# Value-weight sums and second-block x sums traced behind the key products' outputs, and the last token group's residual added on VectorE with plain stores

## The chip, the cores and the metric

The kernel runs on one core of a Trainium2 chip. The metric is the time of one execution on the device, in microseconds (us). Times below are medians over executions. A ratio is the mean time of one kernel's fast runs over the mean of the other's fast runs of the same rounds, so it is not quite the ratio of the medians that are quoted. Each comparison has its 95% interval. An execution's time is longer than the span that its profile shows: by 1.7 us in before. Experiments 9 to 12 ran on another chip than experiments 1 to 8, each beside before.

## The reference, cut to what matters

```python
xn = _layernorm(x)                       # x: 2048 tokens x 1024
s = _A_ref(xn, wqkv, wo)                 # q, k, v projections; attention over 8 dilated keys; wo
g = _silu(_B_ref(xn, w1, w3, w2))        # gated MLP, 1024 -> 3584 -> 1024
return x + s * g
```

Everything outside is bfloat16. The change touches the key and value projections near the start, and `x + s * g` for the last 512 tokens (the last 256 of each of the last two chunks of 512) at the very end.

## The kernel before

Each large product is a 2x2 block product done with seven block products instead of eight. That needs sums of blocks of weights and of x, which VectorE makes beforehand, and sums of outputs, which VectorE makes while it takes the outputs out of PSUM. The kernel keeps four two-bank tiles in PSUM, so an output that is not taken out in time keeps a later product from getting its banks (below, ScalarE's copy waits for such banks until 67.33 us and PE waits 2.6 us for the copy).

```python
def seven(key, A, B, e11, e12, e22, e21, snap=None):
    ...
    pa = bank2(...); mm(pa, a11, b11)            # first product (none if snap holds it)
    pe = bank2(...); mm(pe, s1, t1)              # needs the first weight sum s1
    pb = bank2(...); act_copy(pb, pa)            # ScalarE; pb needs a free bank pair
    sp5 = k4(...);   act_copy(sp5, pe)
    mm(pa, a12, b21); e11(pa)                    # output on ScalarE
    flush()                                      # the leftover product of the group before
    mm(pb, s2, t2); su2 = k4(...); act_copy(su2, pb)
    mm(pe, s4, b22); e12(pe, su2)                # output on VectorE
    mm(pb, s3, t3);  e22(pb, sp5)                # output on VectorE
    pend.append(tail)                            # tail: mm(pb, a22, t4); e21(pb)
```

An output of the second token chunk goes to a buffer `pk` and from there to DRAM. `pk`, `sp5` and `su2` share one ring of four buffers:

```python
def park(t, c, j0, name):                        # t: 0 q, 1 k, 2 v;  c: token chunk
    tl = k4(name, (2, CH), BF16)
    dst = (q_dram, k_dram, v_dram)[t][c, :, j0:j0 + 2, :]
    def fin():
        nc.sync.dma_start(out=dst, in_=tl[:])
    return tl[:], fin

def qkv_copy(t, c, j0):                          # cut; for VectorE outputs:
    anchor["u"] = anchor.get("v")
    anchor["v"] = nc.vector.tensor_add(d, ps[:], a[0][:])
```

`behind(key)` makes the instruction that follows stand, on its own engine, behind the instruction noted under that key. The sums in question stood like this:

```python
def before_v(g):                                 # called after each of the two key groups
    if g > 0:
        return
    for h in I:
        qkv_load(2, h, wv[h])                    # 2 MB of value weights
    tr(3)                                        # transposes of the last x chunk, by DMA
    qkv_sums(*wv, sv)                            # four VectorE sums, need the value weights

qkv_seven(1, 0, wk0, wk1, sk, before_v, snap[2:4])
with behind("u"):
    xn_sums(xT1[0], xT1[1], xT1[2], xT1[3], xs1) # four VectorE sums of the second token block
...
qkv_seven(2, 0, *wv, sv, step)
```

At the end, the product with `wo` comes out in groups `(b, u, dh, gp)` of 256 tokens by 512 columns. The residual x had been copied to the output beforehand, and each group was added to it by an accumulating store on GpSimd's queue, all but one:

```python
def finished(b, u, dh, gp, ps, add=None):
    last = (b, u, dh, gp) == (1, 1, 0, 1)
    ...
    if last:
        for i in I:
            nc.vector.tensor_mul(g[:, i], ps[i], g[:, i])
            nc.vector.tensor_add(g[:, i], g[:, i], xw[0][:, i])
            nc.sync.dma_start(out=..., in_=g[:, i])
        return
    to_bf16(d, ps, add)
    anchor["v"] = nc.vector.tensor_mul(g, d, g)
    nc.gpsimd.dma_start(out=..., in_=g, accum_op=ALU.add)
```

## Time and profile before

| | before |
|---|---|
| median of the first 3 executions | 735.9 us (734.22 to 736.3) |
| span of the profiled execution | 735.9 us (its time: 737.58) |
| PE busy, VectorE busy | 718.5 us, 622.3 us |
| PE idle in 60-80 us, longest wait there | 2.6 us |
| last matmul's end to the end of the span | 8.8 us |

The page's busy line (engine, us, share of the span, instructions) says which engine bounds the kernel:

```profile
PE 718.5 (98%) x3367; PEld 345.9 (47%) x3367; DVE 622.3 (85%) x674; ACT 314.1 (43%) x327; POOL 103.2 (14%) x162
```

PE idles only 17.4 us in all, so a gain must come from those idle stretches, or from stretches in which PE is slow. The list of PE's waits (who waited for whom: us in total, times, longest) starts with the stall in question:

```profile
PE aq L149 <- ACT bq L159: 2.6, 1, 2.6
```

PE waited for ScalarE's copy of the first value product. Why was the copy late? VectorE's timeline around it shows that (start us, us, engine, line, operation, out<-in, count; in brackets the idle time before and what ended it). Lines L316 to L319 are the value sums, L351 the outputs of the key groups:

```profile
53.70 1.23 DVE L351 TENSOR_TENSOR pk<-bq,pq 128x1024 bf16<-128x1024 f32 x1 [0.46 <-PE bq L149]
61.36 1.23 DVE L316 TENSOR_TENSOR wring<-wring 128x2048 f16<-128x2048 bf16 x1 [6.43 <-DMA wring<-in_A_wqkv_dram]
62.62 1.23 DVE L317 TENSOR_TENSOR wring<-wring 128x2048 f16<-128x2048 f16 x1
63.76 1.22 DVE L319 TENSOR_TENSOR wring<-wring 128x2048 f16<-128x2048 bf16 x1
64.89 1.22 DVE L318 TENSOR_TENSOR h_sb<-wring 128x2048 f16<-128x2048 bf16 x1
66.03 1.22 DVE L351 TENSOR_TENSOR pk<-eq,uq 128x1024 bf16<-128x1024 f32 x1
```

PE had finished that `eq` product at about 60.6 us, but VectorE, which took its instructions in the program's order here, first sat 6.43 us waiting for the value weights and then made the four sums. The copy had to wait for the banks of `eq`; ScalarE's timeline names VectorE's output as what ended its wait:

```profile
67.33 1.00 ACT L159 COPY bq<-aq 128x1024 f32<-128x1024 f32 x1 [7.39 <-DVE pk L351]
```

PE's own timeline shows what followed:

```profile
62.13 1.89 PE L149 MATMUL aq<-xT,wring 128*128 128x512 bf16 x8
63.86 1.89 PE L149 MATMUL eq<-xs,wring 128*128 128x512 f16 x8
68.38 3.02 PE L149 MATMUL aq<-xT,wring 128*128 128x512 bf16 x8 [2.63 <-ACT bq L159]
71.19 2.49 PE L149 MATMUL bq<-xs,h_sb 128*128 128x512 f16 x8
```

After the wait, eight matmuls take 3.02 us, where 1.89 is usual. The windows view gives the granted clock of PE for each stretch, third column from the right:

```profile
66.00:68.00 2.00, 0.00 (x0) 0.00 (x0) 2.00 (x3) 0.67 (x1) 0.00 (x0) 1.00 0.73 162
68.00:70.00 2.00, 1.62 (x6) 0.84 (x6) 2.00 (x3) 1.27 (x2) 0.00 (x0) 0.75 1.02 410
70.00:72.00 2.00, 2.00 (x6) 0.73 (x5) 2.00 (x3) 0.57 (x1) 0.00 (x0) 0.50 1.04 395
72.00:74.00 2.00, 2.00 (x10) 1.13 (x9) 0.91 (x1) 0.73 (x2) 0.00 (x0) 0.90 1.05 415
```

The second place is the end. The timeline of the last 11 us, cut to the last matmuls, VectorE's last addition, the last accumulating stores (POOL) and the last plain ones (SPq), and then SyncE's wait before it closes the program:

```profile
724.84 2.51 POOL L952 DMA_DIRECT2D out_dram<-h_sb  x2 [3.23 <-DVE h_sb L951]
...
725.18 1.89 PE L149 MATMUL wb<-wring,oT 128*128 128x512 f16 x8
...
727.84 1.18 POOL L952 DMA_DIRECT2D out_dram<-h_sb  x1 [0.49 <-DVE h_sb L951]
727.94 1.37 SPq L948 DMA_DIRECT2D out_dram<-h_sb  x2
728.50 0.42 DVE L947 TENSOR_TENSOR h_sb<-h_sb,xw 128x512 bf16<-128x512 bf16 x1
```

```profile
SPq L1072 <- DMA out_dram<-h_sb: 4.7, 1, 4.7
```

All arithmetic is done at 728.9, and the span ends at 735.9: 7 us in which stores land and the program is closed.

### The profile page before, as it was taken

To read this page: it belongs to the slowest core of one execution; us is meant where nothing else is said; L and a number is where in the kernel's file an instruction comes from. 1 tells how busy PE (TensorE), PEld (TensorE's weight loads), DVE (VectorE), ACT (ScalarE), POOL (GpSimd) and SP (SyncE) were. 2 spreads that over 40 slices of the span, in tenths; PEclk is the share of its full clock that TensorE was granted. 3 is DMA by queue.
4 is the path that set the end of the run, shared out by engine and by line. 5 is a ranking of instruction groups with operands and counts; after the bars stand their busy time and mean duration, and the time that the engine had idled before them with its cause. 6 is when DMAs were issued, how large, how long until landed. Compare 5 with 4: busy or idle time off the path is not lost.

```text
span 735.9 us, 8786 instructions
## 1 busy us (share of the span) xinstructions
PE 718.5 (98%) x3367; PEld 345.9 (47%) x3367; DVE 622.3 (85%) x674; ACT 314.1 (43%) x327; POOL 103.2 (14%) x162
## 2 busy tenths in 40 slices
PE   8998999999999999999999999999999999999995
PEld 4654665654444444444444444444444444444442
DVE  8996298968798879878989899969859999979973
ACT  5743343446555545654545411124454555020332
POOL 0000000010410010142202010010334000410012
PEclk9999999999999999999999999999999999999998
DMA  9379438866646452467655745459799443754425
GB/s 336 121 187 325 188 145 262 266 204 211 182 162 200 131 185 86 140 190 242 228 172 190 239 158 198 159 180 370 178 282 324 147 135 103 229 183 144 156 26 88
DMA packets 117562, 140.82 MB, mean 191 GB/s; under 512 B 14225, under 2 KB 91025, under 8 KB 116881
## 3 DMA queue, kind: packets, MB, share of 16 engines
q1 hardware_dynamic: 103120, 100.68, 43.7%
q0 software_dynamic: 14400, 39.59, 18.0%
q8 instruction: 26, 0.43, 0.2%
q14 instruction: 16, 0.12, 0.0%
HBM read 98.30 MB, written 39.58 MB: 187 GB/s over the span
## 4 chain that ended last, share of the span: by engine, by line
PE 57%; DVE 19%; issue 14%; DMA 4%; ACT 3%; POOL 2%; POOLq 0%; SPq 0%; DVEq 0%; ACTq 0%
PE bm L149 16%; PE am L149 11%; PE em L149 11%; PE bq L149 6%; DVE pt L410 4%; PE aq L149 4%; PE eq L149 4%; DVE pt L412 2%; DMA wring<-in_A_wqkv_dram 2%; PE db L149 2%; DVE stats L249 1%; DMA t_dram<-wring 1%; PE wb L149 1%; DVE pt L414 1%; POOL out_dram L952 1%
## 5 line engine op out<-in xcount | busy, mean ns | idle before, releaser
L149 PEld LDWEIGHTS <-wring 128*128 128x128 f16 (+1 forms) x1920 | 201.7, 105 | 219.6 <-issue 8.8
L149 PEld LDWEIGHTS <-h_sb 128*128 128x128 f16 (+1 forms) x1088 | 114.1, 105 | 122.1 <-issue 1.7
L149 PE MATMUL bm<-xs,wring 128*128 128x512 f16 x504 | 117.3, 379 | 0.4 <-DVE h_sb L661 0.2
L149 PE MATMUL am<-xT,wring 128*128 128x512 bf16 x336 | 79.5, 379 | 0.2
L410 DVE TENSOR_TENSOR pt<-qt,kT 128x4096 bf16<-128x4096 bf16 x32 | 73.2, 2288 | 0.7
L149 PE MATMUL db<-wring,h_sb 128*128 128x512 f16 x336 | 73.2, 379 | 0.0
L465 DVE TENSOR_TENSOR BC<-Ep,vT 128x2048 bf16<-128x2048 bf16 x56 | 67.0, 1217 | 0.2
L646 DVE TENSOR_TENSOR um<-em,um 128x1024 f32<-128x1024 f32 x28 | 34.2, 1222 | 19.9 <-PE em L149 19.7
L648 ACT ACTIVATE g<-um 128x1024 bf16<-128x1024 f32 x28 | 29.6, 1057 | 49.7 <-DVE um L646 49.7
L149 PE MATMUL da<-wring,h_sb 128*128 128x512 bf16 x224 | 49.2, 379 | 0.0
L451 POOL DMA_DIRECT2D Ep<-pb x64 | 38.1, 603 | 25.4 <-DVE pb L447 18.5
L149 PE MATMUL bm<-h_sb,wring 128*128 128x512 f16 x168 | 39.7, 379 | 0.0
L149 PE MATMUL em<-xs,wring 128*128 128x512 f16 x168 | 39.7, 379 | 0.0
L149 PE MATMUL em<-xT,wring 128*128 128x512 bf16 x168 | 39.7, 379 | 0.0
L412 DVE TENSOR_TENSOR pt<-pt 128x2048 bf16<-128x2048 bf16 x32 | 39.1, 1221 | 0.5
L475 DVE TENSOR_TENSOR oT<-oT,BC 128x2048 bf16<-128x2048 bf16 x32 | 39.0, 1220 | 0.5
L159 ACT COPY bm<-am 128x1024 f32<-128x1024 f32 x28 | 28.0, 999 | 26.1 <-PE am L149 26.1
L159 ACT COPY pm<-em 128x1024 f32<-128x1024 f32 x28 | 28.4, 1013 | 19.2 <-PE em L149 19.2
L159 ACT COPY um<-bm 128x1024 f32<-128x1024 f32 x28 | 28.4, 1013 | 18.6 <-PE bm L149 18.1
L667 ACT CAST g<-bm 128x1024 bf16<-128x1024 f32 x28 | 28.3, 1010 | 17.6 <-PE bm L149 17.6
L351 DVE TENSOR_TENSOR pk<-eq,uq 128x1024 bf16<-128x1024 f32 x12 | 14.7, 1221 | 21.8 <-PE eq L149 14.1
L952 POOL DMA_DIRECT2D out_dram<-h_sb x15 | 18.8, 1387 | 97.9 <-DVE h_sb L951 97.7
(172 smaller groups left out, 976.3 us busy)
## 6 DMA issues: line engine op xcount, KB each, us to landing
wring<-in_B_w_dram SPq DMA_DIRECT2D x61, 512.0 KB, 4.1
wring<-t_dram SPq DMA_DIRECT2D x16, 512.0 KB, 4.4
t_dram<-wring POOLq DMA_DIRECT2D x14, 512.0 KB, 4.1
wring<-in_A_wqkv_dram SPq DMA_DIRECT2D x6, 1024.0 KB, 8.4
wring<-t_dram SPq DMA_DIRECT2D x16, 384.0 KB, 5.3
wring<-in_B_w_dram SPq DMA_DIRECT2D x12, 384.0 KB, 4.3
wring<-in_A_x_dram SPq DMA_DIRECT2D x16, 256.0 KB, 5.5
Ep<-pb POOLq DMA_DIRECT2D x64, 64.0 KB, 4.6
```

The costliest lines, as they stand in the source:

```text
L149: anchor["pe"] = nc.tensor.matmul(ps, lhsT=lhs[k], rhs=rhs[k], start=(first and k == 0), stop=(k == n - 1), skip_group_check=not first,)
L159: nc.scalar.copy(out=out_, in_=in_)
L351: anchor["v"] = nc.vector.tensor_add(d, ps[:], a[0][:])
L410: nc.vector.tensor_mul(p_t[:], q[:], kT[:, :, o:o + CH])
L412: nc.vector.tensor_add(p_t[:, 0:4, :], p_t[:, 0:4, :], p_t[:, 4:8, :])
L451: nc.gpsimd.dma_start(out=pr[c][r:P:NR, :, sq * P:(sq + 1) * P], in_=pb[sq * 32:(sq + 1) * 32, :, :])
L465: nc.vector.tensor_mul(dst, E[:, w, :].unsqueeze(1).to_broadcast([P, n, CH]), vT[:, js, o:o + CH])
L475: nc.vector.tensor_add(A, A, B if w0 else C)
L646: v = nc.vector.tensor_add(su2[:], pe[:], su2[:])
L648: nc.scalar.activation(out=hl["g"][:, :, CH:], in_=su2[:], func=ACTF.Silu)
L667: nc.scalar.copy(out=hl["g"][:, :, 0:CH], in_=pb[:])
L952: nc.gpsimd.dma_start(out=out_rows(out_flat, b, u, dh, gp), in_=g, accum_op=ALU.add)
```

## The change

It means to let VectorE take the second key group's outputs out of PSUM before it does anything that waits for the value weights, and to end the program without accumulating stores. The diff, cut to its core:

```diff
@@ spill stores of x and its sums (x_dram, xs_dram), from 65-75 us to 164-244 us
-                        nc.sync.dma_start(out=d, in_=f)
+                        with behind("sp"):
+                            nc.sync.dma_start(out=d, in_=f)
@@ before_v
-        if g > 0:
-            return
-        for h in I:
-            qkv_load(2, h, wv[h])
-        tr(3)
-        qkv_sums(*wv, sv)
+        if g == 0:
+            for h in I:
+                qkv_load(2, h, wv[h])
+            tr(3)
+        else:
+            with behind("v"):
+                qkv_sums(*wv, sv)
@@
-    with behind("u"):
-        xn_sums(xT1[0], xT1[1], xT1[2], xT1[3], xs1)
+    def step0(g):
+        if g == 0:
+            with behind("v"):
+                xn_sums(xT1[0], xT1[1], xT1[2], xT1[3], xs1)
+        w2_step()
-    qkv_seven(2, 0, *wv, sv, step)
+    qkv_seven(2, 0, *wv, sv, step0)
@@ finished; xw now holds the residual of four groups, and the copies of x to the output shrink to match
+            if b == 0 or gp == 0:
+                ... accumulating store on GpSimd's queue, as before
+            elif (u, dh) != (1, 0):
+                to_bf16(d, ps, add)
+                nc.vector.tensor_mul(g, d, g)
+                nc.vector.tensor_add(g, g, xw[u, dh])
+                nc.sync.dma_start(out=rows_, in_=g)
+            else:
                 for i in I:
-                    nc.vector.tensor_mul(g[:, i], ps[i], g[:, i])
-                    nc.vector.tensor_add(g[:, i], g[:, i], xw[0][:, i])
+                    if i == 0:
+                        nc.scalar.copy(out=d[:, i], in_=ps[i])
+                    nc.vector.tensor_mul(g[:, i], ps[i] if i else d[:, i], g[:, i])
+                    nc.vector.tensor_add(g[:, i], g[:, i], xw[u, dh][:, i])
```

More of the change, by code (lines that the diff above doesn't have):

```diff
@@ L865, in wo @@
         if b == 1:
-            xw[0] = k4("xw", (2, CH), BF16)
-            nc.sync.dma_start(out=xw[0], in_=out_rows(x_flat, 1, 1, 0, 1))
+            xt4 = att_tile((2, 2, 2, CH), BF16, "xw")
+            for u in I:
+                for dh in I:
+                    xw[u, dh] = xt4[:, u, dh]
+                    nc.sync.dma_start(out=xw[u, dh], in_=out_rows(x_flat, 1, u, dh, 1))
         def product(ps, gp, lhs, rhs, first):
@@ L927 @@
     xw = {}
-    copies = [((2 * b + u) * CH, CH, dh) for b in I for u, dh in ((0, 0), (1, 1), (0, 1), (1, 0)) if (b, u, dh) != (1, 1, 0)]
-    copies.insert(0, (3 * CH, 2 * P, 0))
+    copies = [((2 * b + u) * CH, CH // (1 + b), dh) for b in I for u, dh in ((0, 0), (1, 1), (0, 1), (1, 0))]
     def residual():
@@ L938, in finished @@
     def finished(b, u, dh, gp, ps, add=None):
-        last = (b, u, dh, gp) == (1, 1, 0, 1)
         g = g_tile(b, u, dh, gp)
@@ L942, in finished @@
         d = h_sb[:, 16 + 2 * n:18 + 2 * n, CH:]
+        rows_ = out_rows(out_flat, b, u, dh, gp)
         with hp():
-            if last:
-                for i in I:
-                    nc.vector.tensor_mul(g[:, i], ps[i], g[:, i])
-                    nc.vector.tensor_add(g[:, i], g[:, i], xw[0][:, i])
-                    nc.sync.dma_start(out=out_rows(out_flat, b, u, dh, gp)[:, i], in_=g[:, i])
-                return
-            to_bf16(d, ps, add)
-            anchor["v"] = nc.vector.tensor_mul(g, d, g)
-            nc.gpsimd.dma_start(out=out_rows(out_flat, b, u, dh, gp), in_=g, accum_op=ALU.add)
+            if b == 0 or gp == 0:
+                to_bf16(d, ps, add)
+                anchor["v"] = nc.vector.tensor_mul(g, d, g)
+                nc.gpsimd.dma_start(out=rows_, in_=g, accum_op=ALU.add)
+            elif (u, dh) != (1, 0):
+                to_bf16(d, ps, add)
+                nc.vector.tensor_mul(g, d, g)
+                nc.vector.tensor_add(g, g, xw[u, dh])
+                nc.sync.dma_start(out=rows_, in_=g)
+            else:
+                for i in I:
+                    if i == 0:
+                        nc.scalar.copy(out=d[:, i], in_=ps[i])
+                    nc.vector.tensor_mul(g[:, i], ps[i] if i else d[:, i], g[:, i])
+                    nc.vector.tensor_add(g[:, i], g[:, i], xw[u, dh][:, i])
+                    nc.sync.dma_start(out=rows_[:, i], in_=g[:, i])
     x_load(0)
@@ L1008, in before_v @@
     def before_v(g):
-        if g > 0:
-            return
-        for h in I:
-            qkv_load(2, h, wv[h])
-        tr(3)
-        qkv_sums(*wv, sv)
+        if g == 0:
[5 more added lines that the diff above has]
+                qkv_sums(*wv, sv)
     qkv_seven(1, 0, wk0, wk1, sk, before_v, snap[2:4])
-    with behind("u"):
-        xn_sums(xT1[0], xT1[1], xT1[2], xT1[3], xs1)
     step = lambda g: w2_step()
+    def step0(g):
[3 more added lines that the diff above has]
+        w2_step()
     pace["n"] = PACE[0]
-    qkv_seven(2, 0, *wv, sv, step)
+    qkv_seven(2, 0, *wv, sv, step0)
     pace["n"] = PACE[1]
```

## The prediction

> What bounds it now. TensorE. The page's busy table has PE at 718.5 of 735.9 us, so all PE idling is 17.4 us; VectorE is busy 622.3. A table of busy time by 20 us windows puts the idling at the ends and in one place: 3.4 us in 0-20, 2.6 in 60-80, 8.8 after 720, under 1 anywhere else.
>
> The stall at 66-68 us. In VectorE's timeline the sums of the value weights stand ahead of two evictions of the second key group. They wait for the value weights (idle 6.43 us, until 61.36), run four adds of 1.13 us, and only then is the first key output evicted (66.03). Its PSUM bank is what ScalarE's copy of the first value product needs (67.33), and PE waits 2.63 us for that copy. Afterwards PE is slow: eight matmuls take 3.02 us where 1.89 is usual, and the granted clock is 0.75 in 68-70, 0.50 in 70-72, 0.90 in 72-74. From the starts of the next groups this costs 1.7 us more. [...]
>
> What the change does there. By the instruction order, both key evictions now stand ahead of the value sums, and the second block's x sums (four adds) stand behind two value evictions. On PE the leftover key product moves ahead of the value product that needs the first sum. Expected: evictions at 60.6 and 62.3, the first sum at 63.5-64.7; PE works on the first value product until 63.9, on the leftover product until 65.6, then needs the sum, which is there. The stall and the slow clock go: 4.3 to 4.5 us, all on the critical path, since PE is busy without a gap for 80 us after it. The x sums are first read near 90 us and are not late at about 80. The spill stores of x and its sums leave 65-75 us, where DMA share is 1.02-1.05, for about 190-250 us, where it is about 0.6; I expect nothing of that on PE.
>
> The tail. The last matmul ends at 727.07, VectorE at 728.9; two last stores are issued at 727.94 and 729.0, and SyncE waits until 734.0. In between, three 256 KB accumulating stores keep DMA share at 1.1-1.2 (727-732) and the last store takes 4.9 us to land. The change makes three of the four last groups plain stores: their accumulates go, VectorE gets three more adds of about 0.6 us, ScalarE one copy. Adding up VectorE's queue from 722.1 (1.13 + 2x0.6 for evictions, 0.6 per product or sum), its end moves about 1 us later, to 729.9. But the last store then meets an almost empty queue: plain 256 KB stores land in 2.0-2.4 us at best in this trace. [...] Landing near 732.5 instead of 734.0: gain 1.4 us, uncertain by 0.8. The residual's 1 MB load waits only for the third chunk's last use of its buffer, near 651, and should delay no weights.
>
> Predicted: 735.9 - 4.4 - 1.4 = 730.1 us; 8 in 10 between 728.3 and 732.8. Faster by over 2%: 0.02; within 2%: 0.97; slower: 0.01.
>
> Shown right by: no PE wait for that ScalarE copy, granted clock 1.00 in 60-80, PE busy total near 717, no accumulating store in the last 10 us, last landing 3 us after VectorE's end.
>
> Wrong if: the value weights land later than 62 us; PE then waits for the first sum; evictions on VectorE push the last store past 731; the moved spills delay weights, or a later VectorE-bound stretch (420-490) swallows the lead.

No term of the sum rests on them: 735.9 - 4.4 - 1.4 = 730.1 us stands as recorded. The 4.4 is read from the profile of before (2.63 us of wait and 1.7 of slow matmuls). The 1.4 is an estimate from it: VectorE's queue added up, and the landings of plain 256 KB stores, whose fastest nine of 36 took 2.03 to 2.40 us (the stores of the key, query and value outputs).

## The result, and the profile after

| | before | after |
|---|---|---|
| median of 6 executions | 736.21 us (734.22 to 737.72) | 732.37 us (731.36 to 733.51) |
| ratio, 95% interval | | 0.9949 (0.9932 to 0.9966) |
| span of the profiled execution | 735.9 us | 730.3 us |
| last matmul's end to the end of the span | 8.8 us | 6.0 us |

The time, 732.4 us, lies inside the predicted range, near its upper end. The gain is 3.8 us where 5.8 was predicted. The two profiled spans differ by 5.6 us, so the pair of profiles flatters the change: the profiled execution of before took 737.58 us, 1.4 us above its median.

The busy line after. Some matmul records are missing from this trace (3312 of 3367), so PE's total is a little low:

```profile
PE 714.2 (98%) x3312; PEld 345.8 (47%) x3367; DVE 624.2 (85%) x677; ACT 314.5 (43%) x328; POOL 99.3 (14%) x159
```

The wait for ScalarE's copy is gone from the list of PE's waits, and a small one is new:

```profile
PE bq L149 <- DVE pk L351: 0.3, 1, 0.3
```

VectorE's timeline has the order that was wanted, both key outputs ahead of the value sums. But look at the brackets: neither output started when PE was done. Both waited for a DMA, a store of an earlier key output:

```profile
62.13 1.23 DVE L351 TENSOR_TENSOR pk<-eq,uq 128x1024 bf16<-128x1024 f32 x1 [6.35 <-DMA k_dram<-pk]
63.93 1.23 DVE L351 TENSOR_TENSOR pk<-bq,pq 128x1024 bf16<-128x1024 f32 x1 [0.58 <-DMA k_dram<-pk]
65.07 1.22 DVE L316 TENSOR_TENSOR wring<-wring 128x2048 f16<-128x2048 bf16 x1
```

And PE's timeline. In before, eight such matmuls took 1.73 us from their start to that of the next eight (62.13 to 63.86). By that measure the first value product (`aq`, 62.98) should end 1.73 us after its start, at 64.71; four matmuls of the leftover product start at 65.21, 0.50 us late, and should end 0.86 us later, at 66.07; the next product starts at 66.35, when the first sum is ready, 0.28 us late:

```profile
62.98 1.89 PE L149 MATMUL aq<-xT,wring 128*128 128x512 bf16 x7
65.21 1.02 PE L149 MATMUL bq<-xs,h_sb 128*128 128x512 f16 x4 [0.34 <-DVE pk L351]
66.35 1.92 PE L149 MATMUL eq<-xs,wring 128*128 128x512 f16 x8
```

The granted clock stays at 1.00 (windows view, same columns):

```profile
66.00:68.00 2.00, 1.89 (x10) 0.95 (x9) 1.97 (x3) 0.00 (x0) 0.00 (x0) 1.00 0.95 264
68.00:70.00 2.00, 2.00 (x11) 1.32 (x10) 1.82 (x2) 1.02 (x1) 0.00 (x0) 1.00 0.87 85
70.00:72.00 2.00, 2.00 (x11) 1.09 (x10) 0.00 (x0) 1.93 (x2) 0.00 (x0) 1.00 1.03 388
```

At the end, VectorE finishes 2.8 us after PE (1.9 before), but SyncE waits only 1.2 us for landings, in three pieces (timeline and SyncE's waits):

```profile
722.41 1.89 PE L149 MATMUL wb<-wring,oT 128*128 128x512 f16 x8
...
722.99 3.50 SPq L955 DMA_DIRECT2D out_dram<-h_sb  x3
...
726.34 0.75 DVE L961 TENSOR_TENSOR h_sb<-h_sb,xw 128x512 bf16<-128x512 bf16 x2
726.82 0.84 SPq L962 DMA_DIRECT2D out_dram<-h_sb  x2
```

```profile
SPq L1086 <- DMA out_dram<-h_sb: 1.2, 3, 0.6
```

To compare kernels stretch by stretch, I took five numbers from each trace. A: start of the first query product. B: from the first value product to the first gate product of the MLP, the stretch that holds the stall. C: from there to the first product of the last output stage. D: from the last matmul's end to the end of the span. The last column is the time at half clock before the end. The text below refers to this table.

| profile | A | B | C | D | half clock |
|---|---|---|---|---|---|
| before | 12.41 | 102.15 | 538.4 | 8.81 | 3.41 |
| before, run again | 12.44 | 102.07 | 539.1 | 8.67 | 3.41 |
| new tail only | 12.38 | 100.36 | 539.1 | 6.09 | 0 |
| before without three accumulating stores | 12.71 | 99.76 | 538.6 | 4.68 | 0 |
| later spill stores only | 13.22 | 100.25 | 538.9 | 8.92 | 0 |
| new order only | 13.28 | 99.97 | 539.3 | 7.92 | 0 |
| value sums moved only | 13.04 | 105.12 | 538.3 | 8.50 | 6.83 |
| after | 13.25 | 98.47 | 538.4 | 5.98 | 0 |
| after, run again | 12.91 | 98.88 | 539.6 | 5.97 | 0 |
| after, two additions on GpSimd | 13.32 | 98.84 | 538.6 | 8.16 | 0 |
| after, two stores on GpSimd's queue | 12.92 | 108.28 | 538.6 | 6.08 | 10.24 |
| after, outputs in own memory | 13.57 | 97.73 | 539.2 | 5.96 | 0 |
| the same, old spill stores | 13.30 | 97.72 | 538.5 | 6.08 | 0 |
| the same as own memory, one accumulating store back | 14.00 | 97.72 | 538.6 | 5.76 | 0 |

C varies by 1.3 us among profiles of kernels that are nearly the same there. One profile can't settle a difference of 1 us in the total; B and D are steadier.

### The profile page after: what moved, and what is told of

It reads as the page before. It is cut to its first block, busy times and chain, and to the rows that moved or that the text cites. A ratio compares the mean times of both kernels' runs of the same rounds, so it can differ in the third digit from the quotient of the medians.

```text
span 730.3 us, 8739 instructions
## 1 busy us (share of the span) xinstructions
PE 714.2 (98%) x3312; PEld 345.8 (47%) x3367; DVE 624.2 (85%) x677; ACT 314.5 (43%) x328; POOL 99.3 (14%) x159
## 4 chain that ended last, share of the span: by engine, by line
PE 71%; DVE 18%; DMA 4%; issue 3%; ACT 3%; SPq 1%; POOL 0%; DVEq 0%; ACTq 0%; POOLq 0%
PE bm L149 17%; PE am L149 11%; PE em L149 11%; PE db L149 7%; PE bq L149 5%; PE de L149 4%; DVE pt L410 4%; PE eq L149 4%; PE da L149 3%; PE aq L149 3%; PE wb L149 2%; DVE pt L412 2%; PE we L149 2%; PE wa L149 2%; DMA q_dram<-pk 1%
## 5 line engine op out<-in xcount | busy, mean ns | idle before, releaser
L661 DVE TENSOR_TENSOR h_sb<-bm,pm 128x1024 bf16<-128x1024 f32 x21 | 25.6, 1218 | 5.3 <-PE bm L149 5.3
```

The source lines that it names most:

```text
L661: anchor["v"] = nc.vector.tensor_add(h[:, :, CH:], pb[:], sp5[:])
```

## The experiments

### 1. Before, run again

No edit. It measures how much executions of one program differ.

> The program of before, under another label: it measures how far executions of one program differ, and gives a second profile of it. Theory A (the profiled run of before was a dear one): its 2.63 us stall let the granted clock fall to one half for some 3 us[...]. Then the ratio is 1.000, the mean granted clock differs between executions (0.994 in the first profile, about 0.997 where the clock held) and the time with it by 1 to 2 us. Theory B (the clock falls in every execution): clock 0.994 in all, and times within 0.5 us for the same clock.

(What A expects is that the clock falls in only part of the executions.)

Measured: 737.87 us against 736.84, ratio 1.0004 (0.9983 to 1.0025). The six executions had mean granted clocks from 0.993 to 0.997, and in three jobs together before ran 39 times with its clock listed. In 13 of them the clock was 0.995 or lower, with a mean time of 738.06 us; in 26 it was higher, with 736.06 us. Part of the clock figure comes from the idle end of the program (half clock from 731.2 to 735.9 us in the profile of before), so the two groups may overlap at 0.996. The share of low clocks differs by job: 8 of 17 and 4 of 11 in two jobs on one chip, 1 of 11 in the third, on another chip. The second profile fell into the low group like the first: its trace has one period of half clock near 68 us, 3.413 us long to the nanosecond, as in the first. Three other programs with the same order of VectorE's key and value work (new tail only, no accumulating stores, later spills only) had none in their profiles, although PE waited for the same copy. Without the fall, B is 100.1 us on the mean of those three; with it, 102.1. So an execution with the fall takes 2.0 us longer, and the fall came in about a third of the executions of before. The half clock itself is not all of it: B less PE's wait is 99.52 and 99.15 us with the fall and 97.83 or 97.84 in the three without, so the half clock costs 1.3 to 1.7 us, and the rest is that the stall was longer in the two (2.8 us on the mean, against 2.3). Theory A holds.

PE was idle for 2.63 and 2.92 us in the two profiles where the clock fell, and for 1.92, 2.42 and 2.53 us in the three where it held. Both half-clock periods were 3.413 us long. Whether the length of the gap or something else decides can't be told from five profiles.

### 2. The new order alone

Edit: the first three hunks of the diff above on the kernel before, with the old tail.

> The reordered sums and the later spill stores alone, with the tail of before. From the two profiles the stretch from 50 to 75 us became 3.7 us shorter. If that part is worth the same in every execution: 732.5 us against 736.2 of before (ratio 0.995), nearly the whole of the measured 3.8 us, and the tail would be worth nothing. If the clock fell only in part of the executions of before, it is worth about 2 us (ratio 0.9973). PE should show the short waits of the changed kernel near 65 us (0.5 and 0.3 us) and the clock 1.00 in 60-80.

Measured: 736.26 us against 736.84, ratio 0.9987 (0.9967 to 1.0008): about 1 us, less than either guess, though the interval holds both no gain and the second guess (0.9973). The clock held, as expected (0.996 to 0.998 in all six). But PE's wait for the eviction was 1.6 us in this profile, where it was 0.3 in the profile of the whole change, so B was 99.97 and not 98.5. This made the wait for the earlier stores' landings a suspect: it differs from run to run, and so do the landings: the two stores landed 8.76 and 5.29 us after their issue in before, 7.88 and 5.88 in after.

### 3. The new tail alone

Edit: the last hunk of the diff alone, with the old order.

> The new tail alone, with the old order of the sums. In the two profiles the time from PE's last matmul to the end went from 8.8 to 6.0 us. Theory: the three accumulating stores kept the queues full and the last store late, so this holds in every execution: 2.8 us less (ratio 0.9962), VectorE's end 2.8 us after PE's, the last stores landing in about 1.8 us. Rival: the 4.9 us landing of before was that one run's luck, and 1 to 1.5 us (ratio 0.998 to 0.9985) is what the tail is worth. The stall at 66 us must stay at about 2.6 us.

Measured: 735.13 us against 736.84, ratio 0.9968 (0.9945 to 0.9992), about 2.4 us. D fell to 6.09 us, VectorE ended 2.80 us after PE and the stall was 2.5 us. The ratio's interval holds the rival's 0.998 too; what the rival falls by is D, which is 7.9 to 8.9 us in five profiles with the old tail. With experiment 2, the parts add up to 3.3 us, against 3.8 for the whole, inside the intervals.

### 4. Two outputs in memory of their own

Edit, on the kernel after: the two outputs that waited go to a piece of `oT` that is idle then, not to the ring of four buffers.

```diff
-        tl = k4(name, (2, CH), BF16)
+        if (t, c) == (1, 1) and j0 in (2, 6):
+            tl = oT[:, 0, j0 // 3:j0 // 3 + 2, :]
+        else:
+            tl = k4(name, (2, CH), BF16)
```

> The changed kernel, with the two key results that waited for the landing of two earlier key stores written to a piece of memory of their own (idle at that time) in place of the ring of four buffers. Theory: those landings held both evictions up by 0.7 us and cost PE 0.5 us before the leftover key product and 0.3 us before the product that needs the first value sum. Then VectorE evicts within 0.1 us of PE, both PE waits go, and the kernel is 0.7 us faster than the changed kernel: about 731.7 against 736.2 of before (ratio 0.9939). Rival: the first sum then waits for the weights' landing instead, and PE's waits stay at 0.5 us or more.

Measured: 732.71 us against 736.84, ratio 0.9933 (0.9913 to 0.9952). VectorE's timeline now shows both outputs waiting for PE alone, and PE's shows the three groups back to back (63.30, 65.03, 65.92):

```profile
61.85 1.23 DVE L354 TENSOR_TENSOR oT<-eq,uq 128x1024 bf16<-128x1024 f32 x1 [5.75 <-PE eq L149]
63.50 1.23 DVE L354 TENSOR_TENSOR oT<-bq,pq 128x1024 bf16<-128x1024 f32 x1 [0.43 <-PE bq L149]
64.64 1.22 DVE L316 TENSOR_TENSOR wring<-wring 128x2048 f16<-128x2048 bf16 x1
```

```profile
63.30 1.89 PE L149 MATMUL aq<-xT,wring 128*128 128x512 bf16 x7
65.03 1.03 PE L149 MATMUL bq<-xs,h_sb 128*128 128x512 f16 x4
65.92 1.92 PE L149 MATMUL eq<-xs,wring 128*128 128x512 f16 x8
```

B is 97.73 us, 0.74 less than in the first profile of after, and 97.72 in the two other programs that have this edit. The wait for the ring is shown as the cause. Its size in B differs by profile: the three with the whole change and no other wait added (98.47, 98.88 and 98.84) lie 0.7 to 1.2 us above 97.72. That the whole kernel is faster than after by as much can't be read from the two ratios, whose intervals overlap.

### 5. The value sums moved, the x sums not

Edit, on the kernel before: the `before_v` hunk alone.

> Before with the value sums alone moved behind the key evictions; the x sums of the second block and the spill stores stay as in before, so one x sum now stands ahead of the second key eviction and one between the value sums. Theory: what counts is that nothing that waits for the value weights stands ahead of the evictions. Then the clock holds in 60-80, but PE's two short waits near 65 us grow by the 1.1 us of each x sum ahead of them: between 1 and 2.5 us of PE waiting, so a gain over before of 0 to 1 us (ratio 0.9985 to 1.000), less than the order part with both moves (which had 1 us). Rival: the x sums matter nothing, and this equals the order part to 0.3 us.

Measured: 740.76 us against 736.35, ratio 1.0058 (1.0039 to 1.0077): slower by 4.3 us. I had expected a small gain; both guesses were wrong. One x sum (L294) now stands between the two key outputs, and it waits for the transposes of the last x chunk to land (VectorE's timeline):

```profile
61.95 1.22 DVE L351 TENSOR_TENSOR pk<-eq,uq 128x1024 bf16<-128x1024 f32 x1 [6.38 <-DMA k_dram<-pk]
66.75 1.22 DVE L294 TENSOR_TENSOR h_sb<-h_sb 128x2048 f16<-128x2048 bf16 x1 [3.58 <-DMA h_sb<-wring]
67.89 1.22 DVE L351 TENSOR_TENSOR pk<-bq,pq 128x1024 bf16<-128x1024 f32 x1
```

PE waited 4.5 us for that last output, and the trace has 6.83 us at half clock, twice 3.413. So both moves are needed. In before, the same x sum also stands between the two key outputs, but VectorE reached it only at 67.16 us, after the value sums, when the transposes had landed (66.53).

### 6. Two earlier stores on GpSimd's queue

Edit, on the kernel after: the two key stores whose landing the outputs waited for are issued from GpSimd.

```diff
-            nc.sync.dma_start(out=dst, in_=tl[:])
+            (nc.gpsimd if (t, c) == (1, 1) and j0 in (0, 4) else nc.sync).dma_start(out=dst, in_=tl[:])
```

> The changed kernel with the two earlier key stores, whose landings held the evictions up, issued from GpSimd's queue and not behind the weights and transposes in SyncE's. Theory: they landed late (8 and 6 us after issue) because 2 MB of value weights and the transposes stand ahead of them in the same queue; from another queue they land in about 5 us or less, the evictions wait for PE alone and the gain is as with buffers of their own, 0.7 us (about 731.7 to 732). Rival: [...]the landings are no earlier and the two PE waits stay at 0.8 us or more; the value weights may land later too.

Measured: 741.45 us against 736.35, ratio 1.0067 (1.0041 to 1.0093): by the two ratios of after (0.9949, 0.9958) some 8 to 9 us slower than after, not faster. The rival that the landings would be no earlier was closer, but they were much later: 12.4 and 15.9 us from issue to landing, where it was 7.9 and 5.9 in the profile of after. VectorE's timeline shows the two outputs waiting for them:

```profile
66.59 1.23 DVE L351 TENSOR_TENSOR pk<-eq,uq 128x1024 bf16<-128x1024 f32 x1 [11.15 <-DMA k_dram<-pk]
71.80 1.22 DVE L351 TENSOR_TENSOR pk<-bq,pq 128x1024 bf16<-128x1024 f32 x1 [3.99 <-DMA k_dram<-pk]
```

PE waited 8.5 us, with 10.24 us at half clock, three times 3.413. Why the stores landed so much later stays open. The edit did more than change a queue: with no store ahead of them on SyncE, the four transposes of the last x chunk were issued from 50.17 us on, where it was 54.52 in after, and they landed late too (66.5 to 76.7 us, where it was 62.7 to 66.6). From 54 to 72 us the DMA engines moved 173 GB/s, where it was 298, at a busy share of 1.21 against 1.07. So this run does not tell the queue from the order. As a second proof of experiment 4 it serves: the later the earlier stores land, the longer PE waits (62.01 and 63.81 us and a listed wait of 0.3 in after; 66.5 and 71.7 us and 8.5 here).

### 7. Two of the additions on GpSimd

Edit, on the kernel after:

```diff
-                nc.vector.tensor_add(g, g, xw[u, dh])
+                (nc.vector if (u, dh) == (0, 0) else nc.gpsimd).tensor_add(g, g, xw[u, dh])
```

> The changed kernel with two of the three residual additions of the last token group on GpSimd in place of VectorE. Theory: the end of VectorE's queue sets the end of the program (end comes 3.2 us after it in both profiles with the new tail), so taking two additions of 0.6 us off it ends the program about 1.2 us earlier: end 4.8 us after PE's last matmul where it was 6.0, ratio to before 0.9933. Rival: GpSimd needs 1.5 us or more for an addition and slows VectorE's beside it, so the stores of those two groups become the last to land and the end moves by less than 0.4 us or comes later.

Measured: 735.41 us against 736.35, ratio 0.9994 (0.9977 to 1.0011). After had 0.9949 and 0.9958 in two jobs, so by the ratios this is about 2.6 to 3.3 us worse. D grew from 6.0 to 8.16. The timelines of the two engines at the end:

```profile
722.53 2.12 POOL L954 TENSOR_TENSOR h_sb<-h_sb,xw 128x1024 bf16<-128x1024 bf16 x1 [3.08 <-DVE h_sb L953]
725.32 2.44 POOL L954 TENSOR_TENSOR h_sb<-h_sb,xw 128x1024 bf16<-128x1024 bf16 x1 [0.68 <-PE wb L149]
```

```profile
723.01 2.78 DVE L953 TENSOR_TENSOR h_sb<-h_sb 128x1024 bf16<-128x1024 bf16 x2
725.83 2.49 DVE L954 TENSOR_TENSOR h_sb<-h_sb,xw 128x1024 bf16<-128x1024 bf16 x1
```

GpSimd's additions took 2.12 and 2.44 us. VectorE's addition took 2.49 us beside GpSimd's, 0.68 in after with GpSimd idle; it ended 0.55 us after GpSimd's did, and the product before it likewise (2.18 us, ending 0.55 us after GpSimd's first addition). What held VectorE up is not shown beyond this order of ends. The rival was right that VectorE is slowed and that the end comes later, but the last stores to land were still VectorE's own (731.87 us; those of GpSimd's two groups landed at 726.88 and 730.01). That the end follows VectorE's end is confirmed the hard way: the span ended 3.15 us after VectorE, as in after (3.18).

### 8. Before without the last three accumulating stores

Wrong on purpose: those rows keep the residual alone. Edit, on the kernel before:

```diff
-            nc.gpsimd.dma_start(out=..., in_=g, accum_op=ALU.add)
+            if b == 0 or gp == 0:
+                nc.gpsimd.dma_start(out=..., in_=g, accum_op=ALU.add)
```

> Wrong on purpose: before without the three accumulating stores of the last token group (those rows then keep the residual alone), and everything else as it was. It measures what those stores cost at the end. Theory: the last of them is what the program waits for (its landing some 5 us after its issue, and GpSimd's own drain 0.45 us more); without them the last plain store lands about 2 us after its issue, and the end comes 5.0 to 5.3 us after PE's last matmul in place of 8.7, 3.5 us less (ratio 0.995). Rival: the last plain store was late for another reason, and the end stays above 7 us after PE.

Measured (4 executions): 733.35 us against 736.35, ratio 0.9956 (0.9938 to 0.9975). D fell from 8.8 to 4.68 us, and the two plain stores, the same ones as in before, landed in 1.7 us (median) where it was 4.2 (DMA view, before and then this run: queue, count, KB each, median us to landing):

```profile
out_dram<-h_sb SPq DMA_DIRECT2D x2, 128.0 KB, 4.2
out_dram<-h_sb SPq DMA_DIRECT2D x2, 128.0 KB, 1.7
```

So the accumulating stores were what the end waited for. D with the new tail is 6.0, of which 0.94 us is VectorE's later end (2.80 against 1.86 us after PE); the rest of the difference to 4.68 was not taken apart. In the last 31 us of before, packets of GpSimd's queue took about 117 ns each and those of SyncE's about 48 ns (45.1% of 16 engines' time for 1904 packets against 2.8% for 288); queue and accumulation are not told apart by this.

### 9. After, run again in the rounds of the next three

No edit.

> The changed kernel again, in the same rounds as the next three, so that they can be compared with it: ratio to before 0.993 to 0.997, as first measured (0.9949), the granted clock 0.998 or more in every execution, and some executions of before at 0.995 or less.

Measured: 733.21 us against 736.22, ratio 0.9958 (0.9939 to 0.9977), granted clock 0.998 or 0.999 in all six executions. Only one execution of before in these rounds was below 0.996, so this job saw fewer falls of the clock than the earlier ones. PE's wait for the eviction was 0.7 us in this profile: 0.3, 0.7, 0.7 and 1.6 in four profiles with this order (after, after again, experiment 7, new order only).

### 10. The later spill stores alone

Edit, on the kernel before: the first hunk of the diff alone.

> Before with the later spill stores alone. Theory: the stores of x and its sums are no part of the gain; VectorE's order stands, so the 2.6 us stall stays and the ratio is 1.000 (within 0.0015). Rival: the relief of the DMA queues near 66 us is what helps; then the ratio is 0.998 or less and the wait for ScalarE's copy is shorter.

Measured: 737.17 us against 736.22, ratio 1.0013 (0.9990 to 1.0036). The stall stayed (2.4 us). The stores' new place brings no gain by itself.

### 11. Own memory for two outputs, with the old spill stores

Edit: experiment 4, with the first hunk of the diff taken back.

> The changed kernel with the two key results in memory of their own, and with the spill stores of x and its sums at their old place (near 65 to 80 us). Theory: with nothing on the evictions that waits for a DMA, the spill stores' place is worth nothing: equal to the kernel with the two results in their own memory (0.9933) within 0.001, and PE without a wait of 0.3 us or more between 60 and 80. Rival: the spill stores in the same queue hold up the key and value stores of 70 to 90 us, whose buffers the evictions of the next groups wait for, and PE waits 0.5 us or more between 70 and 100 us.

Measured: 731.87 us against 736.22, ratio 0.9941 (0.9920 to 0.9963). B is 97.72, the same as with the later stores, and PE has no wait above 0.3 us near 70-100 us. In both orders the spill stores' place is worth nothing that can be seen.

### 12. Own memory, and one accumulating store back

Edit: experiment 4, and the earliest of the last groups, `(1, 0, 1, 1)`, accumulates again (its rows of x are copied to the output beforehand again).

```diff
-            if b == 0 or gp == 0:
+            if b == 0 or gp == 0 or (u, dh) == (0, 1):
```

> The changed kernel with the two key results in memory of their own, and with the earliest of the three plain groups of the last token group (second half of the columns, first half of the tokens) stored by an accumulating store again, so that VectorE does one addition less at the end. Theory: that store is issued some 5 us before the end of the others and lands in time, so the end comes 0.5 us earlier after PE's last matmul (5.5 in place of 6.0) and the ratio is about 0.9927. Rival: an accumulating store takes 5 us or more to land and slows the plain stores behind it, so the end stays at 6.0 or comes later.

Measured: 730.96 us against 736.22, ratio 0.9929 (0.9908 to 0.9950), the fastest correct kernel; after had 733.21 in the same rounds. D is 5.76, 0.2 us less than in after, where 0.5 was expected: VectorE's end came 2.52 us after PE, only 0.28 earlier. Three of VectorE's remaining steps, each of which uses the result of the step just before it, then started 0.71 to 0.73 us after that step, where 0.60 is usual there. Of the 2.2 us between the two medians, 0.75 to 1.2 is the wait for the ring (B), 0.2 the tail, and 0.3 lies outside the profiled span (1.74 us against 2.01 on the mean); the rest is not assigned, and C alone varies by 1 us.

## Why the prediction was right or wrong, point by point

**The time was inside the range; the gain was 3.8 us and not 5.8.** The mechanism was right at both places, but four terms of the sum were off. Three cost gain (the clock 1.0 us, the new waits 1.2, the later start 0.65), and the tail gave 1.2 us more than predicted. That the time lies in the range is therefore in part luck: without the tail's 1.2 us it would have been near 733.6 us (an estimate), above the range's 732.8.

**"The stall and the slow clock go: 4.3 to 4.5 us."** They did go. But the 1.7 us for the slow clock was read from one execution and charged to all. The fall came in 13 of 39 listed executions of before, and these took 2.0 us longer on the mean, so it was worth 0.7 us on average (2.0 x 13/39, an estimate over three later jobs, whose shares differ; the clocks of before in the first comparison are not listed). This term was mis-sized by about 1.0 us.

**"Expected: evictions at 60.6 and 62.3 ... PE works on the first value product until 63.9, on the leftover product until 65.6, then needs the sum, which is there."** This step failed. The order was as stated, but the prediction took PE and the weights to be all that the evictions wait for. They also wait for a free buffer of the ring, that is, for stores issued near 54 and 58 us to land (at 62.01 and 63.81 us in after, where the DMA share was 1.02 to 1.22 from 54 to 64 us). In before they landed at 62.03 and 63.98, hidden behind the longer wait, which ended at 66.03. And only four of the eight leftover matmuls were moved ahead of the product that needs the sum, 0.86 us of work and not 1.7. PE waited 0.8 us near 65 us in the profile of after. Experiment 4 took the ring's wait away and B fell by 0.74 us; experiment 6 made it longer and PE waited 8.5 us. Without the clock's fall, B went from 100.1 to 98.7 us (mean of the three profiles with the whole order change and no wait added: 98.47, 98.88, 98.84), a gain of 1.4 us where 2.6 was predicted. Of the missing 1.2 us, 1.0 is this wait (97.72 without it); most of the rest is that the stall of the profiled execution was longer than in those without the fall (2.63 us against 2.29 on the mean).

**"The x sums are first read near 90 us and are not late at about 80" and "I expect nothing of that on PE" of the spill stores.** Right: no PE wait appears there, and experiments 10 and 11 show no effect of the spill stores. What the prediction did not say is that the value sums' move alone loses 4.3 us (experiment 5).

**"Landing near 732.5 instead of 734.0: gain 1.4 us, uncertain by 0.8."** Under-sized, but in the direction it said. VectorE's end moved 0.94 us later, as predicted (1 us). The landing was mis-sized: D went from 8.6 us (mean of five profiles with the old tail) to 6.0, a gain of 2.6 us. The prediction took the last plain store to be what SyncE waits for at 734.0. The trace has SyncE's wait on a pair of semaphores, one of them that of the last accumulating store, and GpSimd's own drain lasting from 727.81 to 735.10 us; the last accumulating store landed at 734.19, 6.35 us after its issue, and the last plain one at 733.85; experiment 8 shows that without the accumulating stores the same plain stores land in 1.7 us. The plain stores of after land in 1.8 to 2.3 us.

**Not foreseen: the first product starts later.** A is 12.4 us in both profiles of before and 13.25 and 12.91 in those of after. PE waits there for layer-normed rows, whose x tiles land later: the fourth x tile is issued at 2.21 us in before and in after, and lands at 5.85 and 6.96. A also differs between other programs (12.38 to 14.00), and follows this landing (it is 6.3 to 6.6 us after it in all 14 profiles). It takes some 0.65 us from the gain in the profiles; why the tile lands later stays open.

The terms together, as estimates from the table and the counts: 1.4 (stall, less the new waits) + 0.7 (clock) + 2.6 (tail) - 0.65 (start) = 4.05 us. The 0.3 us outside the span takes it to the measured 3.8. So close an agreement is luck: the interval of the ratio alone is 1.3 us to either side.

**Signs named beforehand.** No wait for the copy, granted clock 1.00 in 60-80, no accumulating store in the last 10 us (the last was issued at 717.65, 12.6 us before the end): all seen. PE was busy for 718.0 us in the second profile of after, which has all its matmul records, where about 717 was named. "Last landing 3 us after VectorE's end": 2 us after it, with the end of the span 3.2 after it. Of the signs of being wrong, one came: PE waited 0.28 us for the first sum, not because the value weights were late (they landed at 58.67) but because of the ring.

## What to carry to other kernels

Before an instruction is moved ahead of another on an engine that takes them in the program's order, as VectorE did here (an output that was ready at about 60.6 us stood behind the value sums until 66.03), list everything that it waits for, free buffers included: the wait that is removed may only have hidden the next one, here a ring of buffers that outgoing stores keep busy (0.7 to 1.2 us of B). A cost read from a single execution is worth its frequency times its size; a short PE stall that sometimes comes with a halved clock (here 3.413 us of it with stalls of 2.63 and 2.92 us, none with 1.92, 2.42 and 2.53; a low mean clock in 13 of 39 executions) should be counted over many executions' mean clock. At the end of a program, ask which store lands last and what kind it is: three accumulating stores cost more here (D 8.8 us with them, 4.7 without) than three more additions on VectorE (its end 0.94 us later).
